# Local attention scores in blocks of 64 queries by 160 keys, and one values transfer per pair of heads

## The chip, the cores and the metric

One core of a Trainium2 chip runs the program. The metric is device time in microseconds, as the median of several runs; one further run was profiled, and its trace is read here. TensorE (PE) multiplies matrices; its weight loads are listed apart as PEld. VectorE is DVE, ScalarE is ACT, GpSimd is POOL. SyncE (SP) issues nearly all the transfers.

## The reference, cut to what matters

```
# B, H, Sl, D = 4, 8, 512, 64; Sg = 32; window = 32; scale = 1/sqrt(D)
k_all = concat([k_g, k_l]); v_all = concat([v_g, v_l])
out_g = sm(scale * q_g @ k_all.T) @ v_all
s_ll = where(abs(pos[:, None] - pos[None, :]) <= window, scale * q_l @ k_l.T, -1e9)
s_lg = scale * q_l @ k_g.T
out_l = sm(concat([s_lg, s_ll])) @ v_all
x = concat([out_g, out_l])            # to (2176 tokens, 512)
x = (silu(x @ w_gate) * (x @ w_val)) @ w_out        # 512 -> 1536 -> 512
out = mish(x @ w_in) @ w_out                        # 512 -> 2048 -> 512
```

Each local query sees the 65 local keys around it and 32 global keys. All of it is float32; the returned array has 2176 tokens (4 x 544).

## The kernel before

The program has two parts. The **attention part** works through 16 pairs of heads (4 batches, 4 pairs each). It is a list of tasks; the string ORDER, one letter a task, says in which order their instructions are written, so each engine's queue has a fixed order and a task that waits holds up what stands behind it on its engine. The first products of the first MoE layer for the token tiles 0 and 1 (tasks F and F2, line 650) and the preparation of six weight pieces are mixed into this part. The **MoE part** (lines 1018 to 1242) follows it on PE without a gap; its order comes from a planner inside the program (`run`) that does not read the attention part's order.

For a pair of heads n the tasks are: `qk` and `v` (transfers on SP's queue, lines 178 to 183 and 202 to 204); A (PE transposes keys and queries, line 212); Ak and Aq (copies to SBUF as `kst` and `qT`); At and Ag (POOL fills the rest of `kst`: the next block's first 64 keys, lines 293 and 294, and the 32 global keys, line 287); S in two halves g = 0, 1 (scores, line 314); M (DVE adds the mask and takes the minimum, line 325); E (ACT exponential, line 332); R (reciprocal); N (normalise, POOL, lines 344 and 346); C (PE transposes the weights); V (copy); D (PE, probabilities by values, lines 378 and 382). GA to GO do the global queries of two pairs (lines 408 to 454). A, S, C and GT each need one of two double PSUM banks.

A float32 matmul is listed as two PE instructions, called passes below. A score block of before is 128 queries by 192 local and 32 global keys: the query blocks start at query 32 ("turned" queries, the first 32 come last), and only 97 of the 224 columns matter for a query. One half of a task S is four such matmuls, which take 64 rows of the array each (one head on rows 0 to 63, the other on rows 64 to 127). Small fillers (`keep_busy`, line 157, 26 matmuls on zeros) stand between the first tasks of PE.

Of the kernel before, what the change touches and what calls it, by code (L numbers as in the profile page):

```python
# [14 lines left out]
NEG = -1.0e30  # L15
# [6 lines left out]
def tile_attn_moe_moe2(  # L22
# [57 lines left out]
    kst_p = pool("kst", 2, early)  # L80
# [11 lines left out]
    mask = e_p.tile([128, 224], F32, name="mask")  # L92
    mask7 = e_p.tile([128, 224], F32, name="mask7")
# [4 lines left out]
    def setup():  # L98
        nc.gpsimd.memset(ident, 1.0)
        nc.gpsimd.affine_select(out=ident, in_=ident, pattern=[[-1, 128]], compare_op=ALU.is_equal,  # L100
                                fill=0.0, base=0, channel_multiplier=1)
        keep_busy(0, 7)
        nc.vector.memset(qgbd, 0.0)
        for t in (vg, vgb):
            nc.vector.memset(t, 0.0)

        nc.gpsimd.memset(mask, 0.0)
        m = mask[:, 0:192]
        nc.gpsimd.affine_select(out=m, in_=m, pattern=[[1, 192]], compare_op=ALU.is_ge,
                                fill=NEG, base=0, channel_multiplier=-1)  # L110
        nc.gpsimd.affine_select(out=m, in_=m, pattern=[[-1, 192]], compare_op=ALU.is_ge,
                                fill=NEG, base=64, channel_multiplier=1)

        nc.gpsimd.tensor_copy(mask7, mask)
        nc.gpsimd.memset(mask7[64:96, 128:192], NEG)
        nc.gpsimd.memset(mask7[96:128, 64:128], NEG)
# [33 lines left out]
    QS, KS, VW, KST, GK = {}, {}, {}, {}, {}  # L150
# [21 lines left out]
    def load_qk(b, hp):  # L172
        hs = slice(2 * hp, 2 * hp + 2)
        qs = qk_p.tile([128, 4, 2, D], F32, tag="qs", name="qs")
        ks = qk_p.tile([128, 4, 2, D], F32, tag="ks", name="ks")
        eng = nc.sync if b or hp else nc.scalar
        for h in range(2):
            nc.sync.dma_start(out=ks[:, :, h], in_=k_l[b, 2 * hp + h].rearrange("(c p) d -> p c d", p=128))  # L178
        for h in range(2):
            eng.dma_start(out=qs[:, 0:3, h],  # L180
                          in_=q_l[b, 2 * hp + h, SG:SG + 384, :].rearrange("(c p) d -> p c d", p=128))
        eng.dma_start(out=qs[0:96, 3], in_=q_l[b, hs, SG + 384:SL, :].rearrange("h p d -> p h d"))
        eng.dma_start(out=qs[96:128, 3], in_=q_l[b, hs, 0:SG, :].rearrange("h p d -> p h d"))
        QS[b, hp], KS[b, hp] = qs, ks
# [7 lines left out]
    def load_vgb(b):  # L192
        nc.sync.dma_start(out=vgb[96:128], in_=v_g[b].rearrange("h p d -> p h d"))

    def load_v(b, hp):

        hs = slice(2 * hp, 2 * hp + 2)
# [12 lines left out]
    def transpose_half(out, src, j):  # L210
# [7 lines left out]
    KINDS = ("qk A gk w Ak+1 Aq At Cq AG AGk Ag S M E AGe GG GA GGe+1 Cf GM R vg v vgb N Ak GE GR GN C V "  # L218
             "Ch GT GV D AGk+1 Aq+1 GO Xc GXc+1 Xd GV+1 Cl Xc+1 GXh+1 Xh Xh+1 Xl GXl V+1 Ch+1 GXd F_v "
             "F_g GXc Ft Fg Fp Fh Fl Fh+1 GXl+1 F2 Fy Fy+1 GXh Xl+1").split()  # L220
    ORDER = "abcdaefgchaijkllmkmmmmmmnnnnibopedcnqgnramsnntbskfelfhluvammmmmmmmwnxnnngyybizgsAnBCkfDEDEnqsslmmFnnGcHm"
    ORDER += "muwnntlbnIemnnJAyayKmmmigDEDoBslkCEalpLkmmmmmnMnnumnGnnnmNmnnnIyywOwPbaQRDznESfOqDlsuyETUlmmmmmmmmnnnnyI"
    ORDER += "DDnrnnEngVVkWdtLXbwAlMefIusYZcmvOlmmQmgnUnnBbmmmM01ayymzhsnnf2DDnEEnCdqlssscgVGwnIUHamnmlummMVtnSAnyWyk1"
    ORDER += "YmmmmnnnnnUb0zxKOZaDXQiiDBlEjhul3Immm4kCyg1mmmmmVb5nnnnnnnnDsLefyEGwuoRTHl6DqEpy2lmOnmnmymnSgsbekkrfImmm"
    ORDER += "nnmDZwOadaE7nWns1tsYcDlgLEQVlmmAmmbInnnnu3eRmmyyqkmmKlUnn2D0wvVRBnEtDC4mmm00USWgVncm5GnuEhnnlOwy1s8xiHbd"
    ORDER += "7msmmyAnIefaDnnsmEn13nBCilsnMDjou0LyyEmmmml4wOGnnnngphmmmZkPrIDmw5Dnnnn0uEEbUlYssImeOMOmmmfUn2SqskyyVaDD"
    ORDER += "sZaELgEtlFQQlMImnnVkmmmm9TAnmBmmbVCnM2nnn!!xzufnnn#ylb!y!emmnnnSm#n6Km#gkwvwDDXX17gnZlOOddulmm$UIqWyymmm"
    ORDER += "mmmtGD1nnnnnnnnEu0P3ADVl45EL6lwIwmmnmnnmnyyBmmm7mNZnnnnDCuD!My!OREyXUGI%DU9PDEL$#X&VI2%9OMTOMUZ!!$$O&&"
# [36 lines left out]
    def add_pair(n):  # L265
# [15 lines left out]
        def kst():  # L281
            if (b, hp) not in KST:
                KST[b, hp] = kst_p.tile([128, 4, 224], F32, tag="kst", name="kst")
            return KST[b, hp]

        def glob_keys():
            nc.gpsimd.tensor_copy(kst()[:, :, 192:224], GK[b, "kT"][:, hp:hp + 1, :].to_broadcast([128, 4, SG]))

        def keys():
            duplicate(("Ak", n), kst()[:, :, 0:128].rearrange("c r (j t) -> c r j t", j=2), R["pk"])  # L290

        def more_keys():
            nc.gpsimd.tensor_copy(kst()[:, 0:3, 128:192], kst()[:, 1:4, 0:64])
            nc.gpsimd.tensor_copy(kst()[:, 3, 128:192], kst()[:, 0, 0:64])
# [15 lines left out]
        def scores(g):  # L310
            p = both(("S", n, g))
            for pp in range(2):
                for h in range(2):
                    nc.tensor.matmul(p[:, h, 224 * pp:224 * pp + 224], lhsT=R["qT"][half(h), 2 * g + pp, :],  # L314
                                     rhs=KST[b, hp][half(h), 2 * g + pp, :], start=True, stop=True)

        def minimum(g, i):
            if "sm" not in R:
                R["sm"] = sm_p.tile([128, NB, 224], F32, tag="sm", name="sm")
# [6 lines left out]
                out=R["sm"][:, x], in0=both(("S", n, g))[:, h, 224 * pp:224 * pp + 224],  # L326
                in1=mask7 if 2 * g + pp == 3 else mask, scale=-scale, scalar=3.0e38,
# [12 lines left out]
        def normalise(g):  # L340
# [3 lines left out]
            eng.tensor_tensor(out=sm[:, i0:i1, 0:192], in0=sm[:, i0:i1, 0:192],  # L344
                              in1=r.unsqueeze(2).to_broadcast([128, 4, 192]), op=ALU.mult)
            eng.tensor_tensor(out=R["sng"][:, i0:i1, :], in0=sm[:, i0:i1, 192:224],
# [4 lines left out]
        def turn(g):  # L351
            p = both(("C", n, g))
            for k in range(4):
                for j in range(2):
                    transpose_half(p[:, j, 64 * k:64 * k + 64], R["sm"][half(j), 4 * g + k, 64 * j:64 * j + 128], j)
# [8 lines left out]
        for g in range(2):  # L364
            task(("S", n, g), "PE", [("Aq", n), ("At", n), ("Ag", n)], lambda g=g: scores(g), 2, ("M", n, g, 3))
# [8 lines left out]
        def values():  # L374
# [5 lines left out]
            for i in range(NB):  # L380
                for h in range(2):
                    nc.tensor.matmul(p[half(h), 64 * i:64 * i + 64], lhsT=vw[:, i, h, :],  # L382
# [15 lines left out]
    def add_glob(u):  # L398
# [6 lines left out]
        def scores():  # L405
            for e in range(2):
                lq = qgbd[:, 2 * up + e].rearrange("c h r -> c (h r)")
                nc.tensor.matmul(one(("GA", u))[half(e)], lhsT=lq, rhs=KST[b, 2 * up + e][:, :, 0:128],  # L408
# [9 lines left out]
        def exponential():  # L418
            sg = R["sg"] = g_p.tile([128, S], F32, tag="sg", name="sg")
# [16 lines left out]
        def turn():  # L436
            p = both(("GT", u))
            for c in range(5):
                c0 = 128 * c if c < 4 else S - 128
                for e in range(2):  # L440
                    transpose_half(p[:, e, 64 * c:64 * c + 64], R["sg"][half(e), c0:c0 + 128], e)
# [30 lines left out]
    def add_batch(b):  # L472
# [31 lines left out]
        task(("AGk", b), "DVE ACT", [("AG", b, 0)] + prev(("Ag", HP * b - 1), ("GG", b - 1)), keys)  # L504
# [32 lines left out]
    def attention():  # L537
# [12 lines left out]
        steady = iter("040202002030020013")  # L550
# [159 lines left out]
    def out_rows(c0, n):  # L710


        parts = [(b * SL + lo, hi - lo, b * S + r) for b in range(B)
                 for lo, hi, r in ((0, SL - SG, 2 * SG), (SL - SG, SL, SG))]
        parts += [(B * SL + b * SG, SG, b * S) for b in range(B)]
        for at, k, r in parts:
            a, e = max(c0, at), min(c0 + n, at + k)
            if a < e:
                yield a - c0, r + a - at, e - a

    def out_rows(c0, n):


        parts = [(b * SL + lo, hi - lo, b * S + r) for b in range(B)
                 for lo, hi, r in ((0, SL - SG, 2 * SG), (SL - SG, SL, SG))]
# [715 lines left out]
```

## Time and profile before

| | us |
|---|---|
| median of 3 runs (lowest to highest) | 891.88 (891.61 to 892.87) |
| the profiled run, whole | 890.72 |
| its span, first to last instruction | 889.0 |
| first matmul of the MoE part in it | 158.97 |

The time of the profiled run is its span and 1.7 us around it. PE is listed as busy for 877.6 of 889.0 us, but ends of matmuls are modelled and a waiting matmul counts as busy, so that share says little on how full PE is; the chain that ended last and the weight loads say more.

### The profile page before, as it was taken

How to read it: one execution, taken by the hardware profiler on the slowest of the kernel's cores; microseconds unless marked ns; L12 is line 12 of the kernel's file. 1: busy time of each engine (PE TensorE's matmuls, PEld its weight loads, DVE VectorE, ACT ScalarE, POOL GpSimd, SP SyncE). 2: the span in 40 equal slices, each digit the busy share in tenths (PEclk: the TensorE clock that was granted, in tenths of full speed). 3: DMA queues.
4: the chain of work that ended last, by engine and by line, in shares of the span. 5: the costliest groups of instructions: out<-in, count | busy, mean ns of one | idle time of the engine just before them, and what ended most of it. 6: DMA issues, size and time to landing. Idle time of an engine off the chain costs nothing.

```text
span 889.0 us, 17205 instructions
## 1 busy us (share of the span) xinstructions
PE 877.6 (99%) x6252; PEld 808.0 (91%) x6252; DVE 649.6 (73%) x1224; ACT 490.8 (55%) x1177; POOL 541.3 (61%) x550
## 2 busy tenths in 40 slices
PE   7999999999999999999999999999999999999998
PEld 6777888988999999999999999998989898989896
DVE  5777786779777888778778899777777777753434
ACT  6888886454435454455455678764445444544341
POOL 4798887699964386375374799564454436633231
PEclk9999999999999999999999999999999999999999
DMA  7777775577555646646546335664737374726283
GB/s 167 169 182 168 189 173 147 197 233 240 195 190 197 224 148 209 205 139 230 178 153 221 137 142 194 224 222 156 250 116 261 121 263 139 259 80 197 61 266 144
DMA packets 165334, 164.19 MB, mean 185 GB/s; under 512 B 81793, under 2 KB 143745, under 8 KB 165249
## 3 DMA queue, kind: packets, MB, share of 16 engines
q1 hardware_dynamic: 163824, 162.24, 57.8%
q8 instruction: 49, 0.80, 0.4%
q10 hardware_dynamic: 1424, 0.85, 0.3%
q14 instruction: 37, 0.30, 0.1%
HBM read 136.31 MB, written 26.74 MB: 183 GB/s over the span
## 4 chain that ended last, share of the span: by engine, by line
PE 94%; DMA 2%; SPq 1%; DVE 1%; ACT 0%; issue 0%; ACTq 0%; DVEq 0%
PE p L1127 37%; PE p L1232 21%; PE p L1018 15%; PE p L1084 8%; PE one L650 3%; PE pair L212 2%; PE pair L314 2%; PE one L378 1%; PE one L382 1%; DMA qs<-in_q_l 1%; PE one L454 1%; DMA gkq<-in_q_g 1%; PE one L408 1%; DMA vw<-in_v_l 0%; SPq L178 0%
## 5 line engine op out<-in xcount | busy, mean ns | idle before, releaser
L1127 PE MATMUL p<-xh,w 128*128 128x384 f32 (+1 forms) x992 | 258.3, 326 | 0.0
L1232 PE MATMUL p<-w,a 128*128 128x512 f32 x816 | 194.3, 391 | 0.0
L1232 PEld LDWEIGHTS p<-w,a 128*128 128x128 f32 x816 | 152.2, 188 | 29.9
L1127 PEld LDWEIGHTS p<-xh,w 128*128 128x128 f32 x992 | 176.9, 188 | 1.4
L1127 PE MATMUL p<-xl,w 128*128 128x384 f32 (+1 forms) x496 | 161.5, 326 | 0.0
L1139 ACT ACTIVATE b<-p 128x384 f32<-128x384 f32 (+1 forms) x144 | 68.0, 472 | 158.1 <-PE p L1127 153.7
L1018 PE MATMUL p<-a,w 128*128 128x384 f32 (+2 forms) x768 | 142.8, 334 | 0.0
L1048 POOL TENSOR_TENSOR a<-b,a 128x384 fp32r<-128x384 f32 (+1 forms) x58 | 62.0, 1068 | 117.9 <-ACT a L1046 76.6
L1018 PEld LDWEIGHTS p<-a,w 128*128 128x128 f32 x768 | 130.5, 188 | 2.8
L1242 DVE TENSOR_TENSOR y<-p,y 128x512 f32<-128x512 f32 x119 | 82.1, 690 | 65.3 <-PE p L1232 63.8
L880 POOL TENSOR_TENSOR w<-cx,w 128x256 fp32r<-128x256 f32 (+1 forms) x90 | 100.0, 1119 | 44.4 <-ACT w L879 38.9
L833 DVE TENSOR_TENSOR b<-p,b 128x384 f32<-128x384 f32 (+1 forms) x144 | 76.3, 531 | 64.2 <-PE p L1127 42.9
L1048 POOL TENSOR_TENSOR a<-s,a 128x384 fp32r<-128x384 f32 (+2 forms) x53 | 61.5, 1161 | 65.8 <-ACT a L1046 65.8
L1127 PE MATMUL p<-e,w 128*128 128x384 f32 (+1 forms) x528 | 101.3, 328 | 0.0
L1127 PEld LDWEIGHTS p<-xl,w 128*128 128x128 f32 x496 | 93.1, 188 | 1.5
L1127 PEld LDWEIGHTS p<-e,w 128*128 128x128 f32 x528 | 90.0, 188 | 1.0
L1027 DVE TENSOR_TENSOR y<-p,y 128x384 f32<-128x384 f32 (+2 forms) x116 | 62.5, 542 | 22.7 <-PE p L1018 21.3
L1084 PE MATMUL p<-xh,w 128*128 128x384 f32 (+1 forms) x256 | 72.6, 355 | 0.0
L1046 ACT ACTIVATE a<-s 128x384 fp32r<-128x384 f32 (+2 forms) x88 | 45.4, 516 | 47.0 <-DVE s L1070 45.9
L591 DVE SCALAR_TENSOR_TENSOR fl<-q,st 128x512 f32<-128x512 f32 x68 | 62.4, 918 | 9.8 <-ACT q L583 9.6
L595 DVE SCALAR_TENSOR_TENSOR cx<-fl,cx 128x512 uint32<-128x512 uint32 x68 | 65.9, 969 | 0.5
L332 ACT ACTIVATE sm<-sm,nb 128x224 f32<-128x224 f32 x128 | 60.0, 473 | 3.7 <-DVE nb L325 3.6
(153 smaller groups left out, 1512.9 us busy)
## 6 DMA issues: line engine op xcount, KB each, us to landing
e<-td SPq DMA_DIRECT2D x76, 384.0 KB
xh<-td SPq DMA_DIRECT2D x38, 384.0 KB
xl<-td SPq DMA_DIRECT2D x38, 384.0 KB
st<-in_moe_w_out SPq DMA_DIRECT2D x28, 512.0 KB
st<-in_moe_w_in SPq DMA_DIRECT2D x16, 512.0 KB
vw<-in_v_l SPq DMA_DIRECT2D x32, 224.0 KB
e<-td SPq DMA_DIRECT2D x20, 320.0 KB
st<-in_moe_w_gate SPq DMA_DIRECT2D x12, 512.0 KB
```

The lines of the kernel that those rows point to most:

```text
L591: nc.vector.scalar_tensor_tensor(fl, q, TINY2, hw, op0=ALU.is_ge, op1=ALU.mult)
L595: nc.vector.scalar_tensor_tensor(x, fu, 0xC0000000, x, op0=ALU.bitwise_and, op1=ALU.bitwise_or)
L833: return lambda e: vec(e).tensor_tensor(out=out(), in0=a(), in1=b(), op=op)
L880: add(lo or [("POOL", PO(n))], 0, lambda e: vec(e).tensor_tensor(out=dst(1), in0=src(), in1=dst(0).bitcast(F32), op=ALU.subtract), r=[rd, ...
L1018: nc.tensor.matmul(ps.h[:, 0:n], lhsT=a.h[:, d], rhs=b.h[:, at:at + n], start=(i == 0 and j == 0), stop=(i == len(ws) - 1 and j == 2))
L1027: add("DVE", DV(n), lambda e: nc.vector.tensor_tensor(out=ya, in0=ps.h[:, 0:n], in1=ya, op=ALU.add), r=[ps], w=yt)
L1048: t.append(add(either(n), 0, lambda e: vec(e).tensor_tensor(out=dst(1), in0=get(), in1=dst(0).bitcast(F32), op=ALU.subtract), r=[v, (av[0] ...
L1084: nc.tensor.matmul(ps.h[:, 0:n], lhsT=a.h[:, d], rhs=b[:, c, c0:c0 + n], start=(c == 0 and j == 0), stop=(c == KD - 1 and j == 2))
L1127: nc.tensor.matmul(ps.h[:, 0:n], lhsT=w.h[:, 256 * a + 128 * c:256 * a + 128 * c + 128], rhs=xs[b][:, c, :], start=(start and c == 0 and j ...
L1139: add("ACT", AC(n), lambda e: nc.scalar.activation(out=dst.h[:, 0:n], in_=src.h[:, 0:n], func=AF.Copy), r=[sv], w=[dst])
L1232: nc.tensor.matmul(ps.h, lhsT=a.h[:, d], rhs=b.h, start=(i == 0 and q == 0), stop=(i == len(ws) - 1 and q == 2))
L1242: add("DVE", DV(512), lambda e: nc.vector.tensor_tensor(out=ya, in0=pa(), in1=ya, op=ALU.add), r=[ps], w=tok)
```

## The change

- Score blocks are 64 queries by 128 local and 32 global keys. Queries are not turned: block i has queries 64i to 64i + 63 and keys 64i - 32 to 64i + 95. Keys lie in one row `KT` with 32 zero columns at each end, so that a window is a slice of it. POOL's copies (tasks At, Ag) are gone; the global keys are read from where they lie, by a matmul of their own.
- One half of S becomes 16 matmuls: for each of four blocks two heads by 128 columns, then two heads by 32 columns. Each takes a quarter of the array (64 rows by 64 columns).
- M, E and N work on 160 columns in place of 224 (N: 4 x 128 in place of 4 x 192), with a mask for the first and one for the last blocks.
- The queries of a head come in one transfer (4 for 6 a pair with the keys), the values of both heads in one transfer of 16 windows (1 for 4, but for the first and the last pair). A transfer for `vgb` is added per batch. The global queries' buffer `SGT` gets 32 zero columns in front.
- ORDER and KINDS are new; `keep_busy` has 15 matmuls for 26; the global keys have two buffers. Copies are shared out anew: 12 of 32 copies V on DVE (6 before), 9 of 16 casts Xh (4 before), 3 of 32 tasks N (none before).
- Output rows follow the new token order, in fewer transfers.

```diff
-    ORDER = "abcdaefgchaijkllmkmmmmmmnnnnibopedcnqgnramsnntbskfelfhluvammmmmmmmwnxnnngyybizgsAnBCkfDEDEnqsslmmFnnGcHm"
+    ORDER = "abacdbeffghijjjgkijjijjjjjjdljijjjmmmmmmmmnopmmmmmafajqrmmfsskkmtupvvvvwxyotwzziiABybbjjjjjCjDjjaawdwdEu"
...
-            eng.dma_start(out=qs[:, 0:3, h],
-                          in_=q_l[b, 2 * hp + h, SG:SG + 384, :].rearrange("(c p) d -> p c d", p=128))
-        eng.dma_start(out=qs[0:96, 3], in_=q_l[b, hs, SG + 384:SL, :].rearrange("h p d -> p h d"))
-        eng.dma_start(out=qs[96:128, 3], in_=q_l[b, hs, 0:SG, :].rearrange("h p d -> p h d"))
+            eng.dma_start(out=qs[:, :, h], in_=q_l[b, 2 * hp + h].rearrange("(c p) d -> p c d", p=128))
...
-        vw = v_p.tile([128, NB, 2, D], F32, tag="vw", name="vw")
-        for h in range(2):
-            v = v_l[b, 2 * hp + h]
-            windows = bass.AP(v.tensor, v.offset, [[D, 128], [64 * D, NB - 1], [1, D]])
-            nc.sync.dma_start(out=vw[:, 0:NB - 1, h], in_=windows)
-        nc.sync.dma_start(out=vw[0:64, NB - 1], in_=v_l[b, hs, SL - 64:SL, :].rearrange("h p d -> p h d"))
-        nc.sync.dma_start(out=vw[64:128, NB - 1], in_=v_l[b, hs, 0:64, :].rearrange("h p d -> p h d"))
+        vw = v_p.tile([128, 2, NB, D], F32, tag="vw", name="vw")
+        flat = vw.rearrange("p h i d -> p (h i) d")
+        v = v_l[b, 2 * hp]
+
+        def windows(x0, x1, r0, r1):
+            at = v.offset + (64 * x0 - SG + r0) * D
+            nc.sync.dma_start(out=flat[r0:r1, x0:x1], in_=bass.AP(v.tensor, at, [[D, r1 - r0], [64 * D, x1 - x0], [1, D]]))
+
+        first, final = (b, hp) == (0, 0), (b, hp) == (B - 1, HP - 1)
+        windows(int(first), 2 * NB - int(final), 0, 128)
...
-            p = both(("S", n, g))
+            p, keys = both(("S", n, g)), KT[n % 2]
             for pp in range(2):
-                for h in range(2):
-                    nc.tensor.matmul(p[:, h, 224 * pp:224 * pp + 224], lhsT=R["qT"][half(h), 2 * g + pp, :],
-                                     rhs=KST[b, hp][half(h), 2 * g + pp, :], start=True, stop=True)
+                r = 2 * g + pp
+                for j in range(2):
+                    i = 2 * r + j
+                    for h in range(2):
+                        nc.tensor.matmul(p[half(j), h, 160 * pp:160 * pp + 128], lhsT=R["qT"][half(h), r, half(j)],
+                                         rhs=keys[half(h), 64 * i:64 * i + 128], start=True, stop=True)
+                    for h in range(2):
+                        nc.tensor.matmul(p[half(j), h, 160 * pp + 128:160 * pp + 160], lhsT=R["qT"][half(h), r, half(j)],
+                                         rhs=GK[b, "kT"][half(h), hp, :], start=True, stop=True)
...
-            task(("S", n, g), "PE", [("Aq", n), ("At", n), ("Ag", n)], lambda g=g: scores(g), 2, ("M", n, g, 3))
+            task(("S", n, g), "PE", [("Aq", n), ("Ak", n), ("AGk", b)], lambda g=g: scores(g), 2, ("M", n, g, 3))
...
-        steady = iter("040202002030020013")
+        steady = iter("030100010003")
```

On PE, a place late in the attention part of before: both halves of one pair's scores (one row), that the values product of another pair follows. The names are the tile written and the tiles read; `128x224` is the tile of the result.

```order
L454 MATMUL one_119<-gtl,vgb 64x32 x2
L314 MATMUL pair_118<-kst,qT 128x224 x4
L378 MATMUL one_122<-pt,vg 64x128 x8
L382 MATMUL one_122<-pt,vw 64x64 x16
L212 MATMUL pair_117<-ident,sm 128x64 x8
```

The same place after the change. The two rows L317 and L320 are one block of queries, and stand four times in one half of S.

```order
L317 MATMUL pair_119<-kt_113,qT 64x128 x2
L320 MATMUL pair_119<-gkT,qT 64x32 x2
L460 MATMUL one_122<-gtl,vw 64x32 x8
L460 MATMUL one_122<-gtl,vgb 64x32 x2
L384 MATMUL one_120<-pt,vg 64x128 x8
L388 MATMUL one_120<-pt,vw 64x64 x16
L226 MATMUL pair_118<-ident,sm 128x64 x8
```

Four matmuls of 224 columns on half arrays became eight of 128 and eight of 32 columns on quarters, in program order block by block.

On SP's queue, the values of the first two pairs in before, from the queries of pair 4 to the values of pair 1:

```order
L180 DMA qs<-in_q_l 128x3x64 x2
L182 DMA qs<-in_q_l 96x2x64
L183 DMA qs<-in_q_l 32x2x64
L202 DMA vw<-in_v_l 128x7x64 x2
L203 DMA vw<-in_v_l 64x2x64
L204 DMA vw<-in_v_l 64x2x64
L193 DMA vgb<-in_v_g 32x8x64
```

After the change the same queue, from the queries of pair 3 to the values of pair 1:

```order
L188 DMA qs<-in_q_l 128x4x64 x2
L194 DMA vg<-in_v_g 32x4x64 x4
L209 DMA vw<-in_v_l 128x15x64
L209 DMA vw<-in_v_l 96x64
L215 DMA vw<-in_v_l 32x64
L209 DMA vw<-in_v_l 128x16x64
```

Ahead of the end of the queries of pair 3 stood 28 issues on SP and now stand 19 (with them); ahead of the end of the first pair's values 42 and now 26.

## Rows read from the trace of the kernel before

**Rows 1.** The profile page: the chain that ended last, by engine.

```profile
PE 94%; DMA 2%; SPq 1%; DVE 1%; ACT 0%; issue 0%; ACTq 0%; DVEq 0%
```

**Rows 2.** Busy time per stretch; columns as the first row says, then clock, DMA share.

```profile
core 0: us, PE busy (x) PEld busy (x) DVE busy (x) ACT busy (x) POOL busy (x), PEclk, DMA share, GB/s
0.00:30.00 30.00, 25.07 (x284) 19.74 (x286) 17.49 (x75) 21.52 (x67) 16.04 (x40) 1.00 0.72 166
30.00:90.00 60.00, 57.32 (x928) 46.02 (x926) 45.34 (x176) 50.46 (x164) 51.85 (x65) 1.00 0.73 177
90.00:159.00 69.00, 69.00 (x1070) 58.81 (x1067) 51.30 (x173) 53.21 (x170) 53.90 (x63) 1.00 0.67 167
159.00:889.00 730.00, 726.17 (x3984) 683.47 (x3982) 535.45 (x802) 365.62 (x777) 419.49 (x385) 1.00 0.56 188
```

**Rows 3.** The chain from 120 us on: start, us, what (instructions).

```profile
127.81 0.96 PE pair L314 x8
...
135.97 1.02 PE one L378 x16
136.99 0.93 PE one L382 x32
137.92 0.86 PE one L408 x4
...
142.29 0.81 PE pair L314 x8
143.10 1.29 PE one L454 x40
...
158.97 14.56 PE p L1084 x84
```

**Rows 4.** The chain from 0 to 30 us: start, us, what.

```profile
1.31 3.71 DMA qs<-in_q_l
...
11.93 0.64 PE one L157 x4
...
15.52 3.70 DMA qs<-in_q_l
...
24.84 0.86 PE one L157 x6
```

**Rows 5.** SP's queue in order of time: start, us, line, transfer (issues).

```profile
16.69 1.32 SPq L183 DMA_DIRECT2D qs<-in_q_l  x1
...
23.10 1.04 SPq L202 DMA_DIRECT2D vw<-in_v_l  x2
24.18 0.68 SPq L203 DMA_DIRECT2D vw<-in_v_l  x1
24.91 0.61 SPq L204 DMA_DIRECT2D vw<-in_v_l  x1
```

**Rows 6.** Groups of instructions, 0 to 159 us (fillers: to 200): busy us, mean ns, idle before.

```profile
L157 PEld LDWEIGHTS one<-zeros 128*128 128x128 f32 x52 | 7.9, 229 | 2.2 <-DVE zeros L153 1.1 <-issue 0.8
L325 DVE CUSTOM_DVE_ANT_0 sm<-pair,mask 128x224 f32<-128x224 f32 x128 | 42.6, 385 | 21.4 <-PE pair L314 16.0 <-PE pair L212 1.7 <-POOL sng L346 1.7
L421 ACT ACTIVATE sg<-one,grc 128x512 f32<-128x512 f32 x8 | 5.4, 681 | 0.0
L423 ACT ACTIVATE sg<-gg,grc 128x32 f32<-128x32 f32 x8 | 2.5, 318 | 0.0
L344 POOL TENSOR_TENSOR sm<-sm,rc 128x768 f32<-128x768 f32 x32 | 48.3, 1508 | 11.2 <-DVE rc L338 8.0 <-ACT xf L235 2.4 <-ACT pt L235 0.9
L346 POOL TENSOR_TENSOR sng<-sm,rc 128x128 f32<-128x128 f32 x32 | 14.2, 444 | 0.0
L293 POOL COPY kst<-kst 128x192 f32<-128x192 f32 x16 | 6.7, 419 | 10.6 <-ACT kst L235 9.6 <-DVE kst L237 1.0
L287 POOL COPY kst<-gkT 128x128 f32<-128x128 f32 x16 | 4.9, 319 | 2.7 <-DVE gkT L237 1.7 <-PE one L408 0.6 <-PE pair L314 0.3
L294 POOL COPY kst<-kst 128x64 f32<-128x64 f32 x16 | 4.2, 263 | 0.0
```

More of the change, by code (lines that the diff above doesn't have):

```diff
@@ L91, in tile_attn_moe_moe2 @@
     ident = e_p.tile([128, 128], F32, name="ident")
-    mask = e_p.tile([128, 224], F32, name="mask")
-    mask7 = e_p.tile([128, 224], F32, name="mask7")
+    mask = e_p.tile([128, 160], F32, name="mask")
+    mask0 = e_p.tile([128, 160], F32, name="mask0")
+    mask7 = e_p.tile([128, 160], F32, name="mask7")
+    KT = [e_p.tile([128, SG + SL + SG], F32, name=f"kt{i}") for i in range(2)]
+    SGT = e_p.tile([128, SG + S], F32, name="sgt")
     qgbd = e_p.tile([128, HP, 2, SG], F32, name="qgbd")
@@ L107, in setup @@
         nc.gpsimd.memset(mask, 0.0)
[L108 to L116, printed above, removed]
+        for j in range(2):
+            m = mask[half(j), 0:128]
+            nc.gpsimd.affine_select(out=m, in_=m, pattern=[[1, 128]], compare_op=ALU.is_ge,
+                                    fill=NEG, base=0, channel_multiplier=-1)
+            nc.gpsimd.affine_select(out=m, in_=m, pattern=[[-1, 128]], compare_op=ALU.is_ge,
+                                    fill=NEG, base=64, channel_multiplier=1)
+        for t in (mask0, mask7):
+            nc.gpsimd.tensor_copy(t, mask)
+        nc.gpsimd.memset(mask0[half(0), 0:SG], NEG)
+        nc.gpsimd.memset(mask7[half(1), 128 - SG:128], NEG)
+        for t in KT:
+            nc.gpsimd.memset(t[:, 0:SG], 0.0)
+            nc.gpsimd.memset(t[:, SG + SL:], 0.0)
+        nc.gpsimd.memset(SGT[:, 0:SG], 0.0)
     XF = {}
@@ L192, in load_vgb @@
     def load_vgb(b):
+        nc.sync.dma_start(out=vgb[64:96], in_=v_l[b, :, SL - SG:SL].rearrange("h p d -> p h d"))
         nc.sync.dma_start(out=vgb[96:128], in_=v_g[b].rearrange("h p d -> p h d"))
     def load_v(b, hp):
-        hs = slice(2 * hp, 2 * hp + 2)
-        vw = v_p.tile([128, NB, 2, D], F32, tag="vw", name="vw")
-        for h in range(2):
-            v = v_l[b, 2 * hp + h]
-            windows = bass.AP(v.tensor, v.offset, [[D, 128], [64 * D, NB - 1], [1, D]])
-            nc.sync.dma_start(out=vw[:, 0:NB - 1, h], in_=windows)
-        nc.sync.dma_start(out=vw[0:64, NB - 1], in_=v_l[b, hs, SL - 64:SL, :].rearrange("h p d -> p h d"))
-        nc.sync.dma_start(out=vw[64:128, NB - 1], in_=v_l[b, hs, 0:64, :].rearrange("h p d -> p h d"))
+        vw = v_p.tile([128, 2, NB, D], F32, tag="vw", name="vw")
[6 more added lines that the diff above has]
+        windows(int(first), 2 * NB - int(final), 0, 128)
+        if first:
+            windows(0, 1, SG, 128)
+            nc.sync.dma_start(out=flat[0:SG, 0], in_=v[0:SG])
+        if final:
+            windows(2 * NB - 1, 2 * NB, 0, 128 - SG)
+            nc.sync.dma_start(out=flat[128 - SG:128, 2 * NB - 1], in_=v[0:SG])
         VW[b, hp] = vw
@@ L279, in qk @@
             R["pk"], R["pq"] = (p[:, :, 256 * i:256 * i + 256].rearrange("c j (r t) -> c r j t", t=64) for i in range(2))
[L281 to L287, printed above, removed]
         def keys():
[L290 to L294, printed above, removed]
+            duplicate(("Ak", n), KT[n % 2][:, SG:SG + SL].rearrange("c (r j t) -> c r j t", j=2, t=64), R["pk"])
         def queries():
@@ L325, in minimum @@
             nc.vector.tensor_tensor_reduce(
-                out=R["sm"][:, x], in0=both(("S", n, g))[:, h, 224 * pp:224 * pp + 224],
-                in1=mask7 if 2 * g + pp == 3 else mask, scale=-scale, scalar=3.0e38,
+                out=R["sm"][:, x], in0=both(("S", n, g))[:, h, 160 * pp:160 * pp + 160],
+                in1=(mask0, mask, mask, mask7)[2 * g + pp], scale=-scale, scalar=3.0e38,
                 op0=ALU.add, op1=ALU.min, accum_out=R["nb"][:, x:x + 1])
@@ L343, in normalise @@
             eng = nc.gpsimd if ON["N", n, g] == "POOL" else nc.vector
[L344 to L346 removed]
+            eng.tensor_tensor(out=sm[:, i0:i1, 0:128], in0=sm[:, i0:i1, 0:128],
+                              in1=r.unsqueeze(2).to_broadcast([128, 4, 128]), op=ALU.mult)
+            eng.tensor_tensor(out=R["sng"][:, i0:i1, :], in0=sm[:, i0:i1, 128:160],
                               in1=r.unsqueeze(2).to_broadcast([128, 4, SG]), op=ALU.mult)
@@ L354, in turn @@
                 for j in range(2):
-                    transpose_half(p[:, j, 64 * k:64 * k + 64], R["sm"][half(j), 4 * g + k, 64 * j:64 * j + 128], j)
+                    transpose_half(p[:, j, 64 * k:64 * k + 64], R["sm"][half(j), 4 * g + k, 0:128], j)
             for j in range(2):
@@ L381, in values @@
                 for h in range(2):
-                    nc.tensor.matmul(p[half(h), 64 * i:64 * i + 64], lhsT=vw[:, i, h, :],
+                    nc.tensor.matmul(p[half(h), 64 * i:64 * i + 64], lhsT=vw[:, h, i, :],
                                      rhs=R["pt", i // 4][:, i % 2, 2 * (i // 2 % 2) + h, :],
@@ L407, in scores @@
                 lq = qgbd[:, 2 * up + e].rearrange("c h r -> c (h r)")
-                nc.tensor.matmul(one(("GA", u))[half(e)], lhsT=lq, rhs=KST[b, 2 * up + e][:, :, 0:128],
+                nc.tensor.matmul(one(("GA", u))[half(e)], lhsT=lq, rhs=KT[e][:, SG:SG + SL],
                                  start=True, stop=True)
@@ L438, in turn @@
             for c in range(5):
-                c0 = 128 * c if c < 4 else S - 128
+                c0 = 128 * c if c < 4 else SG + S - 128
                 for e in range(2):
-                    transpose_half(p[:, e, 64 * c:64 * c + 64], R["sg"][half(e), c0:c0 + 128], e)
+                    transpose_half(p[:, e, 64 * c:64 * c + 64], SGT[half(e), c0:c0 + 128], e)
         def turned():
@@ L503, in add_batch @@
         task(("AG", b, 0), "PE", [("gk", b, 0)], lambda: turn(0), 1, ("AGe", b))
-        task(("AGk", b), "DVE ACT", [("AG", b, 0)] + prev(("Ag", HP * b - 1), ("GG", b - 1)), keys)
+        task(("AGk", b), "DVE ACT", [("AG", b, 0)] + ([("S", HP * (b - 1) - 1, 1), ("GG", b - 2)] if b > 1 else []), keys)
         task(("AG", b, 1), "PE", [("gk", b, 1), ("AG", b, 0)], lambda: turn(1))
@@ L710, in out_rows @@
     def out_rows(c0, n):
[L713 to L725, printed above, removed]
+        parts = [(b * SL, SL, b * S + SG) for b in range(B)]
         parts += [(B * SL + b * SG, SG, b * S) for b in range(B)]
```

34 lines of the change are left out of this document (16 added, 18 removed).

## The prediction

> **What bounds the kernel now.** I read the page first: the chain that ended last is 94% PE [rows 1], so a change can only pay where PE is held up or where PE's own work gets shorter. Then the stretches [rows 2]. From 159 us on the MoE part is PE alone: 726.17 of 730 us busy, and nothing in the change touches its order on PE. So whatever the attention part gains or loses up to the first MoE matmul at 158.97 us [rows 3] goes one to one into the total, and I forecast that point.
>
> Within the attention part, PE's busy share misleads (25.07 of 30, then 57.32 of 60, then 69.00 of 69), since a matmul that waits counts as busy. Weight loads show the work better, as each pass has one. In 90 to 159 us the chain is PE without a break [rows 3] and PEld is busy 58.81 of 69 us, 0.852 [rows 2]. I call that full. In 30 to 90 us it is 46.02 of 60: at the full rate that work takes 46.02 / 0.852 = 54.0 us, so **6.0 us are lost** there. In 0 to 30 us it is 19.74, of which the fillers have 7.9 [rows 6]; the rest, 11.8, takes 13.9 us at the full rate, so **16.1 us are lost**. In all 22 us of the 159 are lost before 90 us. The last 69 us are bound by PE's own passes.
>
> What PE lacked in the lost time is seen in the chain: two loads of queries of 3.7 us each stand in it before 20 us [rows 4]. They were late because SP issues one transfer after another: the last issue for the queries of pair 3 ends at 18.0 us, and the four for the values of pair 0 run from 23.1 to 25.5 us [rows 5].
>
> **The change, part by part.**
>
> *Scores on PE.* This decides. Prices per pass on half arrays, dense: 128 columns (1.02 - 0.15) / 16 = 0.054 us (0.15 us is a switch of tiling, priced below); 64 columns 0.93 / 32 = 0.029 us; 32 columns 1.29 / 40 = 0.032 us [rows 3]. So 32 columns cost no less than 64. On the full array a filler matmul of 128 columns (two passes) costs 0.86 - 0.64 = 0.22 us, by a row of six passes and one of four [rows 4]: 0.11 a pass. Half of that on half arrays means that the two halves run side by side, each pass 0.11 us (128 columns) or 0.058 us (64 or 32). A quarter array has no row in this trace. A pass of 128 columns on it I price as 0.11, one of 32 as 0.058, by the half arrays. In one half of S each of the four quarters has 4 wide and 4 narrow passes: 4 x 0.11 + 4 x 0.058 = 0.67 us.
> - Bound below: all four quarters side by side, 0.67 us for one half of S.
> - Two at a time: 1.35 us.
> - Bound above: one at a time, 2.7 us.
>
> Before it is 0.81 us [rows 3]. The 32 halves of S so cost between -0.14 x 32 = -4.5 us and +1.9 x 32 = +60 us. I take 0.72, near the lower end: -0.09 x 32 = **-2.9 us**. The reason is the row L408, 0.86 us for four passes of 512 columns, two on each half of the array [rows 3]. One such pass takes 4 x 0.11 = 0.44 us. Written in the order first half, first half, second half, second half, and begun strictly in that order, they would take three rounds, 1.3 us; they take two. So a pass for a free part of the array goes past one that waits for its own part. Here eight passes of two quarters stand ahead of the first one for the third, and not one; that is why I don't take it as certain.
>
> The Trainium skill ("TensorE: Matmul & The Clock Gate", Part 3, What overlaps and what doesn't) says against this that matmuls start and end strictly in program order, and only weight loads are pulled ahead. The row L408 disagrees with it for float32 passes. By that rule the strict order of rival 1 would hold, 907 us.
>
> *Switches between tilings.* A half of S is 0.81 us behind transposes (the same tiling) and 0.96 behind matmuls on the full array [rows 3]: a switch costs 0.15 us. Counting the neighbours in PE's order there are 107 switches now and 116 after: **+1.4 us**.
>
> *Fillers* go from 26 matmuls to 15, 11 x 0.22 = 2.4 us. They stand in lost time of the first stretch; I count nothing for them.
>
> *Transfers.* 5 issues fewer a pair, at about 0.5 us each (1.04 for two, then 0.68 and 0.61 [rows 5]), is some 40 us of SP's queue over the part. At the start 9 issues fewer stand up to the end of pair 3's queries: these go out 4.5 us earlier. 16 fewer stand up to the first values: 8 us earlier. Bytes and packets stay. A single transfer of 512 KB lands later after its issue than one of 224 KB, but its issue is four times shorter, and it is asked for two pairs ahead; I count no cost.
>
> *Column work.* M per block: 64 columns fewer at about 1 ns each (385 ns for 224 columns bounds it at 1.7 ns) is -0.07 us, -8 us of DVE over 128 blocks. E: slope (681 - 318) / 480 = 0.76 ns, so -48 ns, -6 us of ACT. N: slope (1508 - 444) / 640 = 1.66 ns, 256 columns fewer is -0.43 us, -13 us of POOL; At and Ag (6.7 + 4.2 + 4.9 us) go too [rows 6]. ACT also gives 6 copies V and 5 casts to DVE, which comes out even. None of these engines is full (DVE 51.30, ACT 53.21, POOL 53.90 of 69 us [rows 2]), so this is worth only the shorter path of a pair: no 419 + 263 ns between keys and scores, and -0.43 us in N. It helps in the first 90 us, where such chains hold PE up, and not after it.
>
> *How much of the lost 22 us returns.* Not below 0, if the new order spends it; not above about 12, as the first load lands at 5.0 us (1.31 + 3.71 [rows 4]) and the first softmax has to run before any values product. I take 4 of the 16 at the start, by the loads that come 4.5 us earlier, and 3 of the 6 in the middle: **-7 us**.
>
> *Elsewhere.* The end of the program still is a DVE sum and a transfer after the last matmul; fewer output transfers stand there, and I count nothing.
>
> **Sum.** -2.9 + 1.4 - 7 = -8.5 us: the first MoE matmul at about 150.5 us, the profiled run at 882.2 (from 890.72), the median at 883.4, as the median of the runs is 1.16 above the profiled one. I say **883.5**.
>
> **The rivals.**
> 1. *Quarters run two at a time, or in program order.* A half of S then takes 1.35 us: +0.54 x 32 = +17.3, +1.4 for switches, and the fuller PE loses less, -9: +10, **902 us**, slower. In strict order (each second pass beside the next quarter's first) a block takes three rounds of 0.11 and a last narrow one of 0.058, 0.39, and a half of S 1.55: +23.7 + 1.4 - 9, about 907 us. For it: no row shows a quarter array, and eight passes must be gone past. Against it: L408. It decides from about 1.05 us for a half of S on, where the sum crosses zero.
> 2. *In between*: the third and fourth quarter begin when the first two have started their second or third pass, about 1.0 us for a half: +6 + 1.4 - 8, **891 us**, no change.
> 3. *PE's work shrinks as I say, but the lost time stays*, since copies moved to DVE (12 of 32 V) or the two double PSUM banks hold the pairs up as now: -1.5 us and up to -2 of waits, **889.5 us**.
> 4. *One quarter at a time*: +60 + 1.4 - 10, **943 us**.
> 5. *The lost time shrinks by 12 us*: **878 us**.
>
> **Chances.** Forecast 0.45 (own range 879 to 888), rival 1 0.20, rival 2 0.13, rival 3 0.12, rival 4 0.04, rival 5 0.06. A measurement here can tell 0.2%, 1.8 us, from no change. Faster by more than that: the forecast, rival 5 and about half of rival 3 and a third of rival 2, 0.60. Within: the rest of these, 0.13. Slower: rivals 1 and 4 and some of 2, 0.27. The range takes in the forecast's and most of the first rival's: 877 to 903; outside stay the strict order, rival 4 and part of rival 5.
>
> **What would show it.** In the chain after the change one half of S (rows L317 and L320, 32 passes) at about 0.7 us when dense; 1.35 or more means rival 1. The first MoE matmul at 150 us, give or take 4. PEld's share in 30 to 90 us nearer to that of 90 on, and the chain's first loads of queries ending before 16 us. If POOL's or DVE's rows now end most of PE's waits, rival 3 holds. I am wrong altogether if the MoE part, 730 us now, changes by more than 1 us.

## The result, and the profile after

The changed kernel takes **881.75 us** (median of 4 runs, 880.06 to 881.91) beside 892.01 us of the kernel before (4 runs, 891.61 to 892.87): ratio 0.9879, 95% interval 0.9862 to 0.9896. The profiled execution is the one of 880.06 us. Its page gives the span and, in the chain that ended last, PE with 98%, where PE had 94% [rows 1]:

```profile
span 878.3 us, 18574 instructions
...
PE 98%; ACT 1%; DMA 0%; SPq 0%; issue 0%; DVE 0%; DVEq 0%
```

Busy time per stretch of the kernel after, columns as in [rows 2]:

```profile
0.00:30.00 30.00, 26.14 (x504) 21.67 (x508) 19.19 (x90) 20.55 (x73) 12.38 (x36) 1.00 0.88 195
30.00:90.00 60.00, 59.88 (x1328) 49.64 (x1330) 45.44 (x193) 50.15 (x172) 43.14 (x48) 1.00 0.86 197
90.00:151.00 61.00, 60.84 (x1210) 54.11 (x1205) 43.60 (x166) 45.16 (x150) 29.32 (x34) 1.00 0.64 161
151.00:878.00 727.00, 723.31 (x3968) 680.65 (x3966) 537.70 (x800) 362.68 (x774) 419.39 (x385) 1.00 0.56 189
```

Before 90 us the DMA share went from 0.72 and 0.73 to 0.88 and 0.86: the same bytes arrive earlier. POOL's 51.85 us between 30 and 90 us fell to 43.14. Where the MoE part begins is seen in the chain (start, us, what):

```profile
148.11 14.56 PE p L1078 x84
```

The MoE part starts at 148.11 us, 10.9 us earlier than before [rows 3], and takes 878.3 - 148.1 = 730.2 us where it took 730.0. All of the gain was made in the attention part. The same chain while PE is dense, both halves of one pair's S:

```profile
115.79 0.39 PE pair L317 x8
116.18 0.09 PE pair L320 x6
116.27 0.24 PE pair L317 x7
116.52 0.10 PE pair L320 x5
116.61 0.24 PE pair L317 x7
116.85 0.10 PE pair L320 x5
116.95 0.24 PE pair L317 x7
117.19 0.10 PE pair L320 x5
117.28 1.02 PE one L384 x16
```

Both halves take 117.28 - 115.79 = 1.49 us; a lone half takes 30.77 - 29.95 = 0.82, so a half is 0.67 us and the switch of tiling in front of it 0.15.

```profile
29.95 0.39 PE pair L317 x8
...
30.43 0.24 PE pair L317 x7
30.67 0.10 PE pair L320 x5
30.77 0.65 PE pair L226 x16
```

In before both halves took 1.71, and a lone half behind a switch 0.96 [rows 3], so the second half added 0.75:

```profile
120.53 1.71 PE pair L314 x16
```

SP's queue in the kernel after, in order of time (start, us, line, transfer, issues):

```profile
10.89 1.00 SPq L188 DMA_DIRECT2D qs<-in_q_l  x2
11.99 2.30 SPq L194 DMA_DIRECT2D vg<-in_v_g  x4
14.34 1.39 SPq L209 DMA_DIRECT2D vw<-in_v_l  x2
...
16.24 0.42 SPq L209 DMA_DIRECT2D vw<-in_v_l  x1
...
26.57 0.45 SPq L585 DMA_DIRECT2D st<-in_moe_w_val  x1
```

The queries of pair 3 are issued by 11.9 us (18.0 in before) and the values of pair 0 by 16.2 (25.5) [rows 5]. The chain from 0 to 24 us no longer has a load of queries in it, but a load of global keys and then ACT's exponentials:

```profile
2.63 3.31 DMA gkq<-in_k_g
...
11.33 5.46 ACT sm L338 x26
```

In the middle of the attention part the chain of before has three more loads, 11.6 us together:

```profile
42.18 3.75 DMA vw<-in_v_l
...
62.28 4.38 DMA gkq<-in_q_g
...
84.91 3.50 DMA qs<-in_q_l
```

In the kernel after no load stands in the chain between 24 us and the MoE part. How far each pair has come can be read from the start of its values product D, here D(0), D(7) and the first MoE matmul: 27.1, 89.0 and 158.8 us in before; 22.4, 77.9 and 147.9 us after. So 4.7 us were gained up to D(0), 6.4 between D(0) and D(7), and nothing after that (69.8 and 70.0 us).

### The profile page after: what moved, and what is told of

Its sections match the earlier page's. It is cut to its first block, busy times and chain, and to the rows that moved or that the text cites. A ratio compares the mean times of both kernels' runs of the same rounds, so it can differ in the third digit from the quotient of the medians.

```text
span 878.3 us, 18574 instructions
## 1 busy us (share of the span) xinstructions
PE 870.2 (99%) x6998; PEld 806.1 (92%) x6998; DVE 645.9 (74%) x1245; ACT 478.5 (54%) x1165; POOL 504.2 (57%) x501
## 4 chain that ended last, share of the span: by engine, by line
PE 98%; ACT 1%; DMA 0%; SPq 0%; issue 0%; DVE 0%; DVEq 0%
PE p L1121 38%; PE p L1226 21%; PE p L1012 15%; PE p L1078 8%; PE one L656 4%; PE pair L226 3%; PE pair L317 2%; PE one L384 2%; PE one L388 2%; PE one L460 1%; PE one L414 1%; ACT sm L338 1%; PE pair L320 1%; DMA gkq<-in_k_g 0%; PE one L484 0%; PE one L165 0%
## 5 line engine op out<-in xcount | busy, mean ns | idle before, releaser
L603 DVE SCALAR_TENSOR_TENSOR cx<-st,cx 128x512 uint32<-128x512 uint32 x68 | 62.5, 921 | 0.4
L601 DVE SCALAR_TENSOR_TENSOR cx<-fl,cx 128x512 uint32<-128x512 uint32 x68 | 61.3, 901 | 0.7
```

The costliest lines, as they stand in the source:

```text
L603: nc.vector.scalar_tensor_tensor(x, STG.pop(p)[:, :, 0], 29, x, op0=ALU.logical_shift_right, op1=ALU.bitwise_or)
```

## The experiments

Each kernel was timed against the kernel before, in turn on one chip. Differences to the kernel after are those of the ratios, times 892 us; with intervals of about plus and minus 0.0015 each they are good to some 2 us. A single profiled execution can lie some 3 us beside the median of its kernel.

**1. The kernel before, with its scores alone on quarter arrays** (224 columns as before, each block of 128 queries as two of 64).

```diff
-                for h in range(2):
-                    nc.tensor.matmul(p[:, h, 224 * pp:224 * pp + 224], lhsT=R["qT"][half(h), 2 * g + pp, :],
...
+                for j in range(2):
+                    for h in range(2):
+                        nc.tensor.matmul(p[half(j), h, 224 * pp:224 * pp + 224], lhsT=R["qT"][half(h), 2 * g + pp, half(j)],
...
```

> The kernel before, with its scores alone on quarter arrays: each 128-query matmul of 224 columns becomes two of 64 queries. Forecast's theory (four quarters side by side): a quarter has 2 matmuls of 2 passes of 224 columns in a half of S, 4 x 0.187 = 0.75 us, as on half arrays (0.81), and some nine more switches of tiling at 0.15 us: 892 to 894 us. Rival (two quarters at a time): a half of S takes 1.5 us, +0.7 x 32 = +23 us, about 914.

Measured: 892.99 us (891.28 to 895.12), ratio 1.0009 (0.9999 to 1.002). In its chain both halves and one half of S:

```profile
137.27 1.68 PE pair L315 x32
...
145.27 0.92 PE pair L315 x16
```

1.68 beside 1.71 us of before: with the same columns, four quarters do the work of two halves in the same time. So they run four at once, and smaller tiles by themselves bring nothing. What a half of the scores gains in the changed kernel is then put down to 160 columns for 224; the two together are what that kernel shows.

**2. The changed kernel in the order of before**, with its 26 fillers (the letters of At and Ag, which are gone, taken out of ORDER).

```diff
...
-        steady = iter("030100010003")
+        steady = iter("040202002030020013")
```

> The whole edit, but with the order of before (its two kinds of POOL copies taken out) and its 26 fillers. Theory (shorter work and fewer issues give back lost time by themselves, the order helps to use it): 885 to 888 us. Rival A (all is in the edit): 882. Rival B (all is in the order): 891 to 893.

Measured: 885.19 us, ratio 0.9924 (0.9909 to 0.9939), 4.0 us behind the kernel after. D(0) starts at 28.3 us, and two loads of queries stand in the chain again (3.48 us at 0.79 and 4.40 us at 16.23).

**3. The kernel before in the new order**, with 15 fillers (Ag placed as early as its inputs allow, At right behind Ak, two buffers for the global keys).

```diff
...
-        steady = iter("040202002030020013")
+        steady = iter("030100010003")
```

> The kernel before with the order of after (its POOL copies put in where they first can stand, two buffers for the global keys) and 15 fillers; scores, column work and transfers as before. Theory: the order alone gives little while SP's issues and POOL's work are as they were: 889 to 893 us. Rival (all is in the order): 882 to 885.

Measured: 905.92 us, ratio 1.0162 (1.0144 to 1.0179): 14 us slower than before, where neither expectation had a loss beyond 1 us. The chain between 64 and 91 us shows why:

```profile
68.28 1.43 POOL sm L335
69.71 0.54 POOL sng L337
70.25 1.87 POOL sm L335
72.12 0.82 POOL sng L337
...
73.26 1.59 PE one L641 x6
74.85 1.74 PE pair L305 x16
...
76.71 0.02 POOL kst L278
```

POOL's normalisations (L335, L337) and its copies into `kst` are in PE's path; between 55 and 90 us POOL is busy 28.23 of 35 us. Up to the MoE part PE itself waits 12 us for POOL, 9.6 of them for L335, and 1.6 us for a load. So with windows of 192 keys and with At and Ag, POOL can't follow the new order. In the waits the granted clock falls too (0.83 between 20 and 30 us, 0.66 between 50 and 55). This kernel also keeps the transfers of before, with which the new order loses in experiment 5, and no run gives it the new ones alone: how the 14 us divide is open.

**4. The changed kernel with a half of S written quarter by quarter**: the same 32 passes, but all of one quarter, then all of the next.

```diff
-            for pp in range(2):
-                r = 2 * g + pp
-                for j in range(2):
-                    i = 2 * r + j
-                    for h in range(2):
+            for j, h in ((0, 0), (0, 1), (1, 0), (1, 1)):
+                for pp in range(2):
+                    r = 2 * g + pp
...
```

> After, with the matmuls of a half of S written quarter by quarter: eight passes for one quarter, then eight for the next, and so on. If a pass for a free quarter goes past any number of waiting ones, a half of S stays at 0.67 us and the total at 881 to 882. Rival (only a few may be gone past, and the shipped order just fits): quarters run partly one behind the other, a half of S at 1.3 to 2.7 us, 900 to 945 us in all.

Measured: 911.57 us, ratio 1.0201 (1.0173 to 1.0229). The chain within one half of S:

```profile
143.33 0.27 PE pair L317 x4
143.61 0.09 PE pair L320 x4
143.69 0.27 PE pair L317 x4
143.97 0.09 PE pair L320 x4
```

0.36 us now hold 4 wide and 4 narrow passes, which is two at a time; in the kernel after 0.34 us hold 8 of each. Both halves take 3.31 us (142.89 to 146.20), where they took 1.49: the rival holds. So a pass for a free quarter does go past waiting ones, but not past any number of them: here eight passes of a quarter's own stand ahead of the next quarter's first, sixteen ahead of the third's, and only two quarters work together. In the shipped order eight passes, of two quarters, stand ahead of the third quarter's first, and all four work. Why there is such a limit no run shows.

**5. The changed kernel with its bytes in as many transfers as before**: queries of a head in two, values of a pair in four.

```diff
-            eng.dma_start(out=qs[:, :, h], in_=q_l[b, 2 * hp + h].rearrange("(c p) d -> p c d", p=128))
+            for c0, c1 in ((0, 3), (3, 4)):
+                eng.dma_start(out=qs[:, c0:c1, h],
...
-        windows(int(first), 2 * NB - int(final), 0, 128)
+        cuts = (int(first), NB - 1, NB, 2 * NB - 1, 2 * NB - int(final))
+        for x0, x1 in zip(cuts, cuts[1:]):
+            if x0 < x1:
+                windows(x0, x1, 0, 128)
```

> After, with the same bytes in as many issues as before: queries of a head in two transfers, values of a pair in four. Theory (late loads cost at the start): 9 and 16 issues more ahead of the first places, 4.5 us later there: +3 to +4 us, 885. Rival (they are hidden, as the start waits for ACT's exponentials): 881.5 to 883.

Measured: 892.05 us, ratio 0.9995 (0.9985 to 1.0004): the whole gain is gone, 10.3 us, where both expectations had 4 at most. D(0) is on time (22.7 us), but D(1) starts at 32.7 for 27.9 and D(2) at 46.4 for 38.0. In this execution, 13 us behind the profiled one of the kernel after, the other 5 us are lost between D(3) and D(9), where two loads of queries stand in the chain (2.17 us at 74.72 and 3.06 us at 90.03). On SP the second piece of MoE weights (`in_moe_w_val`; one of `in_moe_w_gate` goes out at the start) is issued at 35.37 us and not at 26.57:

```profile
35.37 0.46 SPq L590 DMA_DIRECT2D st<-in_moe_w_val  x1
```

The stretches around the gap, the granted clock third from the right:

```profile
23.00:27.50 4.50, 2.44 (x58) 2.02 (x54) 2.80 (x18) 2.71 (x14) 2.27 (x3) 1.00 0.65 142
27.50:34.50 7.00, 6.62 (x92) 5.75 (x94) 4.12 (x17) 4.51 (x16) 2.55 (x3) 0.51 0.70 159
34.50:41.00 6.50, 5.02 (x154) 4.60 (x154) 3.07 (x14) 3.61 (x10) 3.09 (x4) 1.00 0.70 176
41.00:45.00 4.00, 4.00 (x49) 2.27 (x51) 2.66 (x14) 3.18 (x13) 1.40 (x1) 0.57 0.60 134
```

PE is busy 2.44 of 4.5 us, and then the granted clock is 0.51, the lower level, for 7 us; again after 5.02 of 6.5. If PE had been at work all that time, the two stretches cost 7.0 x 0.49 + 4.0 x 0.43 = 5.1 us at most. Late loads are paid twice, once as a wait and once as a slower PE.

**6. The changed kernel with POOL's copies put back** (192 and 64 columns of `KT`, each copied onto itself) between key copy and scores.

```diff
...
+        def pool_copies():
+            t = KT[n % 2]
+            for c0, c1 in ((SG, SG + 192), (SG + 192, SG + 256)):
+                nc.gpsimd.tensor_copy(t[:, c0:c1], t[:, c0:c1])
+        task(("At", n), "POOL", [("Ak", n)], pool_copies)
```

> After, with POOL copies of 192 and 64 columns put back between the key copy and the scores of every pair (in place, nothing else changed). Theory (the shorter path from keys to scores counts only in the first 30 us): +0.5 to +1.5 us, 882 to 883. Rival (chains of pairs hold PE up all along): +0.68 us a pair for some ten pairs, +5 and more, 887.

Measured: 885.53 us, ratio 0.992 (0.9907 to 0.9933), 3.7 us behind the kernel after, between the two expectations. D(0) starts at 26.2 us, 3.8 us late, so most of it is lost at the start; by the MoE part it is 5.7 in this execution. The chain ahead of D(0):

```profile
18.37 0.69 DVE kt L242
...
19.11 0.53 POOL kt L299 x2
19.64 1.00 POOL sm L347
20.64 0.81 POOL sng L349
```

The copies themselves are 0.53 us. But the normalisations L347 and L349, for which PE waits, stand behind them on POOL's queue, and the copies stand behind the key copy on DVE: that is the wait, and after it the granted clock is 0.76 between 20 and 27 us.

**7. The changed kernel with 26 fillers for 15.**

```diff
-        steady = iter("030100010003")
+        steady = iter("040202002030020013")
```

> After, with the 26 fillers of before. Theory (they stand in lost time): 0 to +1 us, 881.5 to 883. Rival (PE has no lost time there any more): 11 x 0.22 = +2.4 us, 884.

Measured: 884.11 us, ratio 0.9909 (0.9895 to 0.9923): 2.7 us more, as the rival has it: 11 x 0.22 = 2.4 us of fillers on the path. Beside experiment 2, which has the same fillers, the order is worth 0.9924 - 0.9909, 1.3 us, which the intervals don't tell from nothing.

**8 and 9. One part of experiment 5 each**: only the queries of a head in two transfers (2 issues a pair), only the values in four (3 issues a pair), with the edits shown there.

> The kernel after, with the queries of a head in two transfers for one: 2 issues more a pair, the values as after. With all five issues back the gain of 10 us was gone. Theory: the issues count by their number on SyncE's queue, two of five, so about 4 us more than after, 885 to 887. Rival 1: it is the queries' part, since those loads stood in the chain of waits at 74.72 and 90.03 us (2.17 and 3.06 us each): 889 to 892. Rival 2: a queue with two issues more still keeps ahead, nothing comes late: 881 to 883.

> The kernel after, with the values of a pair in four transfers for one: 3 issues more a pair, the queries as after. Theory: 3 of the 5 issues, about 6 us more than after, 887 to 889. Rival 1: the queries carry the loss, then 882 to 884. Rival 2: the start alone counts (the first two pairs' values, 24 issues ahead of them for 19), then a loss of about 4 us, all of it before the third values product.

Measured: the queries alone 889.12 us, ratio 0.9959 (0.9946 to 0.9973), 7.1 us behind the kernel after; the values alone 882.68 us, ratio 0.9897 (0.9884 to 0.991), 1.6 us, which the intervals don't tell from nothing. So it isn't the number of issues a pair: three cost less than two, and the first rival holds in both. It is what stands behind them. The profiled execution with the queries split is the fastest of its six, 885.84 us, and shows 5.8 of the 7.1 us. In it D(2) starts at 44.0 us for 38.0, and from there to D(15) the distance stays at 6 us: all of it is lost in the first 44 us. (The waits of 2.17 and 3.06 us that the expectation names are those of experiment 5.) The chain there:

```profile
23.27 4.11 DMA gkq<-in_q_g
...
31.45 1.36 SPq L201
32.86 4.32 DMA st<-in_moe_w_val
...
37.21 0.04 ACT q L591
...
37.77 0.69 ACT pt L251
```

The queue itself, SPq, leads up to the global queries and to the weight piece, which is issued at 32.86 us (26.57 in the kernel after, 29.51 with the values split). PE doesn't wait for these weights: its first F task starts at 52.5 us. ACT does, 1.47 us, before it prepares them (L591), and behind that on ACT's queue stand copies V (`pt`), the next thing that PE needs. In experiment 5 it is the same. Ahead of that piece stand on SP the queries of pairs 1 to 5, so 10 issues more and 6.3 us, and the values of two pairs, 6 more and 2.9 us; with both, as in experiment 5, 16 more and 8.8 us. An issue here costs the queue 0.5 to 0.6 us. In before this piece was issued at 12.19 us; the new order puts it behind the queries of pair 5. That it is this piece, and the global queries ahead of it, is read from the chain: no run moves either by itself.

**10. The changed kernel with the first pair ahead of the global keys**, for whose load PE waits 1.62 us before 6.08 us, and its first half of S ahead of the second pair's transposes. On PE:

```diff
-L484 MATMUL one_120<-ident,gkq 128x128
 L226 MATMUL pair_118<-ident,ks 128x64 x8
 L226 MATMUL pair_118<-ident,qs 128x64 x8
+L475 MATMUL one_120<-ident,gkq 128x128
```

> The kernel after with six tasks at the start in another order: the transposes of pair 0 ahead of that of the global keys (for whose load PE waits 1.62 us at 4.5 us), and the first half of S ahead of the transposes of pair 1. Theory: what stands in the chain from 11.33 us is ACT with 5.46 us of exponentials, which begin as soon as the first masks are done, so a first S that runs 1 us earlier moves the start by 0.5 to 1 us: 881 to 881.7. Rival: the exponentials are one batch behind the masks of both pairs, then the time is that of after, 882, within 0.5.

Measured: 881.84 us, ratio 0.9886 (0.9873 to 0.9898). No gain, as the rival has it: ACT's exponentials still stand in the chain as one piece of 5.34 us, from 11.17 us for 11.33.

**11. The changed kernel without the last 8 fillers** (`steady` empty; the 7 ahead of the first transposes stay).

> The kernel after with the 7 fillers ahead of the first transposes alone, 8 of 0.22 us fewer. 11 more cost 2.7 us. Theory: they stand in the path, 8 fewer give 1.8 us, 880. Rival: they keep PE's clock up across the waits of the first 20 us; without them the granted clock falls to half for a stretch of some 3 us in which PE works at half its rate, and the time is 882 or more.

Measured: 880.68 us, ratio 0.9871 (0.9857 to 0.9885). That is 0.7 us less by the ratios, with intervals that overlap, so not shown to be faster. The granted clock is 1.00 over each of the stretches 0 to 30, 30 to 90 and 90 to 150 us, so these 8 fillers aren't needed for it here. D(0) stays where it was (22.5 us): with the fillers gone, the chain between 7.7 and 9.0 us holds copies of keys and queries on ACT and DVE.

**12. The queries in two transfers for the first four pairs alone.**

```diff
+            for c0, c1 in ((0, 3), (3, 4)) if b == 0 else ((0, 4),):
+                eng.dma_start(out=qs[:, c0:c1, h],
...
```

> The kernel after with the queries of a head in two transfers for the first four pairs alone (8 issues more in all, 2 of them on ScalarE's queue); the other twelve pairs as after. All sixteen so cost 7 us, the values' three issues a pair under 1 us. Theory: it is the start, where the queries of pairs 1 to 3 stand ahead of everything else on SyncE's queue and PE is still empty: 886 to 889. Rival: each pair costs its share, then 4 of 16 pairs cost 2 us, 883 to 884, or nothing, and the loss lies in the middle.

Measured: 883.74 us, ratio 0.9909 (0.9894 to 0.9924), 2.7 us behind the kernel after: the rival's number, and not its reason. D(1) and D(2) start 2.8 us late, D(15) 3.6. Six issues more stand ahead of the weight piece, which goes out at 30.59 us, 4.0 late; in the chain of this execution stands not the piece but a load of queries (4.33 us at 25.87). The loss does lie at the start, but it isn't the first four pairs alone: experiment 8 loses 6 us by D(2), and of its other pairs only 4 and 5 have queries ahead of that piece, so the rest is put down to them; no run splits theirs alone. The piece's delay tells how far the queue is behind there, and over the four runs the loss grows with it: 1.6 us for 2.9 late, 2.7 for 4.0, 7.1 for 6.3 and 10.3 for 8.8.

## Why the prediction was right, and by how much its terms were off

The time, 881.75 us for 883.5, is the forecast's own case. The sum said -8.5 us, the trace says -10.9. That it came so near is partly luck: the stretches of scores gave 2.9 us more than their two terms, the lost time 2.8 us less, and about what is left of the miss is the fillers, 2.4 us that were counted as nothing. Counted from the trace, with every stretch of scores as it stands there (25 in before, 20 after) and transposes at 0.64 / 16 = 0.04 us a pass:

| us | to D(0) | D(0) to D(7) | D(7) to MoE | in all | forecast |
|---|---|---|---|---|---|
| stretches of scores | -0.2 | -2.6 | -1.6 | -4.4 | -1.5 |
| fillers, 11 of 0.22 by count | -2.4 | 0 | 0 | -2.4 | 0 |
| transposes that changed their place | -1.0 | -0.2 | +1.3 | 0 | 0 |
| the rest: lost time that came back | -1.1 | -3.6 | +0.5 | -4.2 | -7 |
| in all | -4.7 | -6.4 | +0.2 | -10.9 | -8.5 |

- **Scores: right in mechanism, and the halves near in size by two errors that cancel.** All four quarters work side by side: a half is 0.67 us, the working's lower bound, and I had taken 0.72. But between other halves it was 1.71 - 0.96 = 0.75 in before and not 0.81. So a half shrank by 0.08 us, and 32 of them by 2.6 beside the 2.9 forecast. The switches were counted right: the weight loads of the two traces change tiling 107 and 116 times, 16 and 20 times into scores. The stretches of scores still went from 29.4 to 25.0 us, 4.4 and not 1.5 us: the new order has 20 of them for 25, and some of before hold waits (in its chain both halves take 1.78 us at 31.11 and 1.83 at 67.56, for 1.71). How the 1.8 us beyond the halves divide is open. Rivals 1, 2 and 4 fell with the 0.67. The Trainium skill ("TensorE: Matmul & The Clock Gate", Part 3, What overlaps and what doesn't) has matmuls start and end strictly in program order; by the working's strict order a half would be 1.55 us. The chain disagrees for float32 passes on quarters, as the row L408 had said [rows 3]. But experiment 4 shows that the doubt behind rival 1, that eight passes stand ahead and not one, was a fair one: with another order of the same passes both halves take 3.31 us and not 1.49, and the kernel is slower than before.
- **Fillers: "I count nothing" does not hold in the changed kernel.** Experiment 7 prices 11 of them there at 2.7 us, so their places are no longer empty. What the 11 cost in before is not shown, as no run takes them out of it alone; and of the 15 left, 8 bring nothing sure (experiment 11).
- **Lost time: -7 was right only together with the fillers** (-4.2 - 2.4). The place was off too: of "4 at the start and 3 in the middle" only 1.1 us without fillers came at the start, and 3.6 in the middle. The loads were issued 6 and 9 us earlier (the working had 4.5 and 8), but then ACT takes over: 5.46 us of exponentials in the chain from 11.33 us.
- **Transfers carry the gain.** The working made the 7 us a matter of earlier loads, and experiment 5 shows it: with five issues a pair back nothing is left. Experiment 2 is the other side: merged transfers and narrow blocks in the order of before, fillers and all, keep 6.8 of the 10.8 us. The loss in experiment 5, 10.3 us, is larger than the term: the new order puts a weight piece that ACT waits for behind more issues (12.19 us in before, 35.37 there), and PE's clock falls in the gaps. Which issues count was not foreseen: those of queries, ahead of that piece and of global queries, cost 7.1 us, those of values 1.6, if anything. A larger single landing of the values cost nothing that can be seen.
- **Column work: "worth only the shorter path of a pair" was right in place** (nothing after D(7)), but I put no price on At and Ag beyond their 0.7 us a pair, and experiment 6 gives 3.7 us. Experiment 3 adds that without the narrow blocks and the new transfers the new order costs 14 us, most of it seen as waits for POOL. Rival 3's sign, waits that POOL's rows end, is met there and not in the changed kernel, whose chain has no POOL row up to the MoE part.
- **MoE part:** 730.0 and 730.2 us, as stated. The other signs came too: the first MoE matmul lies within 150 us give or take 4, and PEld's time between 30 and 90 us rose from 46.02 to 49.64 us.

The parts don't add up one by one: issues 10.3, copies 3.7, fillers 2.7 and the scores' 4.4 make 21 us for a gain of 10.9. Taken out singly, each makes the rest wait. How the 10.3 us of experiment 5 divide into waits and clock is open; 5.1 us is the upper bound for the clock in its profiled execution.

## What to carry to other kernels

Count the issues that stand on a queue ahead of the next thing that PE needs, or that an engine needs which PE waits for; what a merged transfer is worth depends on what comes behind it, not on its bytes. A float32 product could here use quarters of the array as fully as halves, as long as the passes for the four quarters were written block by block and not one quarter after the other. A new order of tasks should be judged together with the load of the engines that it leans on: here the same order was 14 us slower on one version, and on the other the 1.3 us that it is worth by itself don't stand out of the noise.

## What the runs showed of the hardware that was not expected

- Going past waiting passes has a limit: both halves of S took 1.49 us with the quarters alternating block by block, 3.31 with one quarter after the other.
- PE's granted clock went to the lower level right behind gaps in which it had little to do: 0.51 after 2.44 us busy of 4.5, and in experiment 6 0.76 on average between 20 and 27 us, behind 3.7 us in which the chain is on DVE and POOL. Such a gap does not always do it: in the first 10 us PE was busy for 7.2 us in experiment 12 and for 7.3 in the kernel after, and the clock was 0.89 in the one and then 0.54 up to 15 us, and 1.00 throughout in the other.
- Without 8 of the 15 fillers the granted clock stayed at 1.00 (experiment 11).
